# Issuing weight loads at the end of each turn, and three steps from scores to values in the first group

## The chip, the cores and the metric

One NeuronCore of a Trainium2 chip. The engines are TensorE (PE, with its weight loads as PEld), VectorE (DVE), ScalarE (ACT), GpSimd (POOL) and SyncE (SP), which in this kernel issues every DMA. The metric is the device time of one execution in microseconds (us); the program is run several times and the median is compared.

## What is computed

The reference is an attention layer followed by a feed-forward layer with two weight matrices.

- Attention: batch 4, 8 heads, 768 tokens, head size 64. Each query sees the keys at a distance under 16, and 24 summary keys, one per block of 32 keys (the maximum over the block; the summary value is the mean). A softmax runs over both kinds of scores together.
- Feed-forward: the heads' outputs give x of 3072 x 512; `h = x @ w_in` (512 x 2048), `g = h * tanh(softplus(h))` (the Mish function), and the result is `g @ w_out` (2048 x 512).

```python
scores_s = scale * np.einsum('bhsd,bhnd->bhsn', q, k_sum)
scores_s = scores_s + np.log(block)
scores_l_m = np.where(mask_l, scores_l, -1000000000.0)
scores_all = np.concatenate([scores_l_m, scores_s], axis=-1)
...
h = x @ w_in
sp = np.where(h > 20.0, h, np.log1p(np.exp(np.minimum(h, 20.0))))
g = h * np.tanh(sp)
return (g @ w_out).astype(np.float32)
```

## The kernel before

**Units.** The attention is cut into 48 units (`todo`, L393): 12 chunks of 256 tokens by 4 pairs of heads. A unit goes through these stages: its keys and queries are loaded (`att_load_keys`: DMA qk, L251, and a POOL copy of the summary keys into the same tile, L252); scores on PE (`att_scores`, L284 or L288/L290), minimum and mask on DVE (L299), exponentials on ACT (L304); `att_normalize` (DVE L313 and L314, POOL L315); `att_transpose` (PE L321, copied from PSUM to SBUF by ACT, L323, as tile pt, of which there is one); `att_values` (PE L339 into x_ps, then ACT splits off the high part xh, L340, and DVE the low part xl, L341). The values of a unit also need `att_load_values`: DMA vw from memory (L258) and a small DMA of the summary values vm into the same tile (L259). The qk tile and the vw tile have two buffers each, so the load for a unit waits on SP until the unit two before it has done its scores (qk) or its values (vw).

**Groups and steps.** The feed-forward layer works on groups of 512 tokens (8 units), 6 in all, each in 16 steps, one per 128 columns of w_in. In step i PE runs `ff_in` (12 matmuls, L353), ACT the Mish function (L360), ACT or DVE the split of its result into ah and al (L369, L371), and two steps later PE runs `ff_out` (12 matmuls, L381).

**Weights.** Weights arrive as 64-bit words, in 16 pieces of two 512 KB DMAs each (`load_weight`, L119), and are turned into a high and a low 32-bit part, piece by piece: `begin_weight` (ACT w_f, L143; DVE L144 and L145), `join_weight` (DVE L154 and L156), in the next turn `upper_weight` (ACT L129) and `lower_weight` (DVE L134). The stage tile that a piece is loaded into has two buffers, and L156 is the last that reads one: the next load but one waits for it. The tile w_f has one buffer, so `begin_weight` waits for the `lower_weight` of the piece before. Before the change `load_weight` is called as the last line of `join_weight`.

**Order.** The order of each engine's instructions is the order in which the program issues them (`manual_schedule`). A first loop of ten turns (u = 0 to 9) runs the attention of the first 8 units, with half of a weight piece per turn: `join_weight` in odd turns, `lower_weight` and `begin_weight` in even ones. In this loop a turn's loads of qk and vw stand after `join_weight`. Then the main loop runs the 96 steps of the feed-forward, with the next group's attention between them: in the first group (steps 0 to 15) the units stand at the even steps 0 to 12 and at step 13 (`at`), one whole weight piece is begun and joined per step up to step 10, and the values of a unit stand two steps after its scores. Steps 4, 6, 8 and 10 also take the key maximum for a new batch (`key_summary`, DVE L220), which frees a buffer for the load vsum (L199); the odd steps behind them reduce it (`value_summary`, DVE L240), send the result out (vm<-vq, L242) and load the next keys (ks, L195). vsum and ks share one buffer.

**PSUM.** From the main loop on, ph (`ff_in`), the two score tiles of a unit, x_ps and pt_ps rotate over the four buffers of one pool (`ps_w`). In the first loop x_ps and pt_ps use another pool.

Of the kernel before, what the change touches and what calls it, by code (L numbers as in the profile page):

```python
# [31 lines left out]
NFC = DFF // P  # L32
# [18 lines left out]
def _as_f32(bits):  # L51
    import struct
    return struct.unpack("<f", struct.pack("<I", bits))[0]
# [3 lines left out]
def fused_kernel(ctx: ExitStack, tc: tile.TileContext, q0, qk, kt, v0, vw, vs, w_in, w_out, out):  # L57
# [39 lines left out]
    def weight_tiles(pool, name, blocks):  # L97
        return [[pool.tile([P, blocks, WP], F32R, name=f"{name}_{w}_{part}") for part in ("hi", "lo")]
                for w in ("in", "out")]
# [14 lines left out]
    def load_weight():  # L114
        if weights:
            w, fc = weights.pop(0)
            t = stage.tile([P, WB, WP], I64, tag="stage", name=f"w{w}_{fc}")
            for k in range(WB):
                nc.sync.dma_start(t[:, k, :], (w_in, w_out)[w][fc + k])  # L119
            loaded.append((w, fc, t))  # L120
# [5 lines left out]
    def upper_weight():  # L126
        if joined:
            w, fc, f = joined[0]
            nc.scalar.copy(piece(w, 0, fc), f)  # L129

    def lower_weight():
        if joined:
            w, fc, f = joined.pop(0)
            nc.vector.tensor_sub(piece(w, 1, fc), f, piece(w, 0, fc).bitcast(F32))  # L134

    def begin_weight():

        if loaded:
            w, fc, t = loaded.pop(0)
            words = t.rearrange("p k f -> p (k f)").bitcast(U32).rearrange("p (f two) -> p f two", two=2)  # L140
            x, high = words[:, :, 0], words[:, :, 1]
            f = ff.tile([P, WB * WP], F32, tag="f", name=f"w{w}_{fc}_f", bufs=1)
            nc.scalar.activation(f, high.bitcast(F32), AF.Copy, scale=2.0 ** -OFFSET)  # L143
            nc.vector.tensor_scalar(out=x, in0=x, scalar1=29, scalar2=None, op0=ALU.logical_shift_right)  # L144
            nc.vector.scalar_tensor_tensor(out=x, in0=high, scalar=SIGN, in1=x,  # L145
                                           op0=ALU.bitwise_and, op1=ALU.bitwise_or)
            begun.append((w, fc, f, x))

    def join_weight():

        if begun:
            w, fc, f, x = begun.pop(0)
            u = f.bitcast(U32)
            nc.vector.tensor_scalar(out=f, in0=f, scalar1=-_as_f32(F32_MAX), scalar2=_as_f32(F32_MAX),  # L154
                                    op0=ALU.max, op1=ALU.min)
            nc.vector.scalar_tensor_tensor(out=u, in0=u, scalar=3, in1=x,  # L156
                                           op0=ALU.logical_shift_left, op1=ALU.bitwise_or)
            joined.append((w, fc, f))
            load_weight()


    begin = ExitStack()
# [30 lines left out]
    def load_key_source(b, hp):  # L193
        ks = sources[b, hp, 0] = stage.tile([P, S], F32, tag="sum", name=f"ks{b}_{hp}", bufs=1)
        nc.sync.dma_start(ks, kt[b, hp])  # L195
# [27 lines left out]
    def first_value_summary(hp):  # L223

        vm = att.tile([KA, P], F32, tag="vm", name=f"vm0_{hp}", bufs=HP)[KW:KA]
        summary[0, hp].append(vm)
        vwt, t = units[0, hp]["v"], units[0, hp]["rest"]
        ps = att_psum(0, f"vm_ps0_{hp}")
        for j in range(NQ + NR):
            nc.tensor.matmul(ps[KW:KA, 0:P], *((blocks[0:KW, j, :], vwt[0:KW, j, :]) if j < NQ else  # L230
                                               (blocks[:, j, :], t[:, j - NQ, :])),
                             start=(j == 0), stop=(j == NQ + NR - 1))
        nc.scalar.copy(vm, ps[KW:KA, 0:P])
        nc.sync.dma_start(vwt[KW:KA], vm.unsqueeze(1).broadcast_to([NB, NQ, P]))
# [20 lines left out]
    def att_load_values(c, hp):  # L255
        b = c // CPB
        vwt = att.tile([KA, NQ, P], F32, tag="vw", name=f"vw{c}_{hp}")
        nc.sync.dma_start(vwt[0:KW], vw[c, hp].rearrange("p (s k) -> p s k", s=NQ))  # L258
        nc.sync.dma_start(vwt[KW:KA], summary[b, hp][1].unsqueeze(1).broadcast_to([NB, NQ, P]))  # L259
        units[c, hp]["v"] = vwt  # L260

    def att_summaries(u):

        for i, f in ((u, value_summary), (u + 1, load_key_source)):
            if i < len(todo) and todo[i][0] % CPB == 0:
                f(todo[i][0] // CPB, todo[i][1])

    def att_psum(c, name, scores=False):

        pool, tag = (ps_o, "o") if c < CG and not scores else (ps_w, "w")  # L270
        return pool.tile([P, 512], F32, tag=tag, name=name)
# [45 lines left out]
    def att_transpose(c, hp):  # L317
        u = units[c, hp]
        ps = att_psum(c, f"pt_ps{c}_{hp}")
        for s in range(NQ):  # L320
            nc.tensor.transpose(ps[:KA, s * P:(s + 1) * P], u["p"][:, s, :], ident)  # L321
        pt = att.tile([KA, NQ, P], F32, tag="pt", name=f"pt{c}_{hp}", bufs=1)
        nc.scalar.copy(pt.rearrange("p s q -> p (s q)"), ps[:KA, :])  # L323
        u["pt"] = pt

    def att_values(c, hp):
        u = units.pop((c, hp))
        g, half = divmod(c, CG)
        if g not in xs:
            xs[g] = (xp.tile([P, HP, TG], F32R, tag="xh", name=f"xh{g}"),  # L330
                     xp.tile([P, HP, TG], F32R, tag="xl", name=f"xl{g}"))
        xh, xl = (x[:, hp, half * CH:(half + 1) * CH] for x in xs[g])
        ps = att_psum(c, f"x_ps{c}_{hp}")
        for s in range(NQ):
            for h in range(2):
                d = slice(h * D, (h + 1) * D)
                x = ps[d, s * QT:(s + 1) * QT]
                pt = u["pt"][:, h * NQ // 2 + s // 2, s % 2 * QT:(s % 2 + 1) * QT]
                nc.tensor.matmul(x, u["v"][:, s, d], pt, start=True, stop=True)  # L339
        nc.scalar.copy(xh, ps[:, :CH])  # L340
        return lambda: nc.vector.tensor_sub(xl, ps[:, :CH], xh.bitcast(F32))  # L341
# [51 lines left out]
    todo = [(c, hp) for c in range(NCH) for hp in range(HP)]  # L393
    steps = [(g, fc) for g in range(NG) for fc in range(NFC)]

    at = {}
    for u, unit in enumerate(todo[CG * HP:]):
        g, u = divmod(u, CG * HP)
# [17 lines left out]
    for u in range(n + 2):  # L416
        if u % 2 == 0:
            upper_weight()
        if u < n:
            att_scores(*todo[u])  # L420
        if u < HP:
            first_value_summary(u)
        lower = att_values(*todo[u - 2]) if 2 <= u else None
        if u % 2:
            join_weight()
        else:
            lower_weight()
            begin_weight()
        if u + 1 < HP:
            key_summary(0, u + 1, units[todo[u + 1]]["k"][:, WIN:])  # L430
        if lower:
            lower()
        if u == HP + 1:
            begin.close()
            late += weight_tiles(ctx.enter_context(tc.tile_pool(name="late", bufs=1)), "w_late", NFC - EARLY)
        if u < n:
            att_normalize(*todo[u])
        if HP - 2 <= u < n:
            att_load_keys(*todo[u + 2])
        if HP <= u:  # L440
            att_load_values(*todo[u])
        if 1 <= u <= n:
            att_transpose(*todo[u - 1])

    load_key_source(1, 0)
    waiting = []
    for i in range(len(steps) + 2):
        upper_weight()  # L450
        if i < len(steps):
            ff_in(*steps[i])
            ff_act(*steps[i])
            if i < NFC:
                waiting.append(ff_split(*steps[i]))
        if 0 < i <= NFC:
            waiting.pop(0)()
        lower_weight()
        lower = att_values(*at[i - 2]) if i - 2 in at else None
        if lower and i >= NFC:  # L460
            lower()
        if i in at:
            att_scores(*at[i])
        begin_weight()
        if lower and i < NFC:
            lower()
        if NFC <= i < len(steps):
            ff_split(*steps[i])()
        if i in at:
            att_normalize(*at[i])  # L470
        join_weight()
        if i in at:
            if todo.index(at[i]) + 2 < len(todo):
                att_load_keys(*todo[todo.index(at[i]) + 2])
        if i - 2 in at and todo.index(at[i - 2]) + 2 < len(todo):
            att_load_values(*todo[todo.index(at[i - 2]) + 2])
        if i - 1 in at:
            att_summaries(todo.index(at[i - 1]) + 2)
        if i >= 2:
            ff_out(*steps[i - 2])  # L480
        if i - 1 in at:
            att_transpose(*at[i - 1])
# [44 lines left out]
```

## Time and profile before

| | before |
|---|---|
| median of 3 runs | 690.5 us (688.78 to 691.71) |
| profiled execution, its own time | 691.24 us |
| its span, first to last instruction | 689.5 us |
| mean granted TensorE clock | 0.967 |
| PE busy | 641.1 us (93%) |
| DVE, ACT, POOL busy | 290.6, 332.9, 68.1 us |
| chain that ended last, by engine | PE 79%, DMA 6%, ACT 6%, DVE 5% |
| DMA | 71.05 MB, mean 103 GB/s |

Times within the span count from its first instruction. An idle time is put down to what released the engine last; idle time of an engine off the chain costs nothing. A granted clock of 1.00 is 2.4 GHz, 0.50 is 1.2 GHz; a value between them is a mean over the stretch. SPq is SP's queue: its rows are the issues of DMAs, not their transfers, and an issue that must wait for an engine holds all issues behind it.

### The profile page before, as it was taken

How to read it: one execution, taken by the hardware profiler on the slowest of the kernel's cores; microseconds unless marked ns; L12 is line 12 of the kernel's file. 1: busy time of each engine (PE TensorE's matmuls, PEld its weight loads, DVE VectorE, ACT ScalarE, POOL GpSimd, SP SyncE). 2: the span in 40 equal slices, each digit the busy share in tenths (PEclk: the TensorE clock that was granted, in tenths of full speed). 3: DMA queues.
4: the chain of work that ended last, by engine and by line, in shares of the span. 5: the costliest groups of instructions: out<-in, count | busy, mean ns of one | idle time of the engine just before them, and what ended most of it. 6: DMA issues, size and time to landing. Idle time of an engine off the chain costs nothing.

```text
span 689.5 us, 10881 instructions
## 1 busy us (share of the span) xinstructions
PE 641.1 (93%) x4160; PEld 513.9 (75%) x4160; DVE 290.6 (42%) x836; ACT 332.9 (48%) x722; POOL 68.1 (10%) x119
## 2 busy tenths in 40 slices
PE   4845798879999999999999999999999999999997
PEld 3634576667778878878878878878788788888886
DVE  3866889895223225453232244442242232221112
ACT  2655776668555445454554554454464454111111
POOL 3121011021101001001001001001001000000000
PEclk9866899999999999999999999999999999999999
DMA  8776455744232122542112134432141110010001
GB/s 281 197 259 217 153 190 212 213 152 141 59 106 87 45 67 92 158 153 89 45 48 85 44 130 114 134 113 68 45 140 54 45 59 0 1 62 0 1 1 61
DMA packets 31253, 71.05 MB, mean 103 GB/s; under 512 B 4833, under 2 KB 9953, under 8 KB 31201
## 3 DMA queue, kind: packets, MB, share of 16 engines
q1 hardware_dynamic: 31200, 70.35, 31.9%
q8 instruction: 33, 0.54, 0.3%
q14 instruction: 20, 0.16, 0.1%
HBM read 61.54 MB, written 6.29 MB: 98 GB/s over the span
## 4 chain that ended last, share of the span: by engine, by line
PE 79%; DMA 6%; ACT 6%; DVE 5%; issue 2%; SPq 1%; POOL 0%; POOLq 0%; ACTq 0%; DVEq 0%
PE po L381 35%; PE ph L353 34%; PE x_ps L339 4%; PE sc L284 3%; PE pt_ps L321 3%; DVE w_f L156 2%; DMA vsum<-vs 2%; DMA q<-q 1%; DMA v<-v 1%; DVE w_f L154 1%; ACT w_f L143 1%; DMA qk<-qk 1%; ACT pr L304 1%; DMA vw<-vm 1%; ACT L360 1%
## 5 line engine op out<-in xcount | busy, mean ns | idle before, releaser
L360 ACT ACTIVATE a<-ph 128x512 f32<-128x512 f32 x96 | 57.4, 598 | 155.4 <-PE ph L353 155.0
L369 DVE CAST ah<-a 128x512 fp32r<-128x512 f32 x80 | 34.0, 425 | 197.1 <-ACT a L360 197.1
L353 PE MATMUL ph<-xh,w_early_in_hi 128*128 128x512 f32 x240 | 97.8, 407 | 0.0
L381 PE MATMUL po<-w_early_out_hi,ah 128*128 128x512 f32 x240 | 97.5, 406 | 0.0
L360 ACT ACT_TABLE_LOAD x41 | 52.6, 1283 | 88.6 <-PE ph L353 88.4
L353 PE MATMUL ph<-xh,w_early_in_lo 128*128 128x512 f32 x240 | 94.9, 396 | 0.0
L353 PE MATMUL ph<-xl,w_early_in_hi 128*128 128x512 f32 x240 | 94.8, 395 | 0.0
L381 PE MATMUL po<-w_early_out_lo,ah 128*128 128x512 f32 x240 | 94.3, 393 | 0.0
L381 PE MATMUL po<-w_early_out_hi,al 128*128 128x512 f32 x240 | 94.1, 392 | 0.0
L315 POOL TENSOR_TENSOR pr<-pr,rs 128x480 f32<-128x480 f32 x48 | 49.2, 1026 | 394.9 <-DVE rs L314 327.5
L304 ACT ACTIVATE pr<-pr,nm 128x120 f32<-128x120 f32 x192 | 73.5, 384 | 16.8 <-DVE nm L299 16.3
L341 DVE TENSOR_TENSOR xl<-x_ps,xh 128x256 fp32r<-128x256 f32 x48 | 20.3, 423 | 119.8 <-ACT xh L340 119.8
L371 DVE TENSOR_TENSOR al<-a,ah 128x512 fp32r<-128x512 f32 x96 | 66.3, 691 | 2.8
L381 PE MATMUL po<-w_late_out_hi,ah 128*128 128x512 f32 x144 | 58.0, 403 | 0.0
L353 PE MATMUL ph<-xh,w_late_in_hi 128*128 128x512 f32 x144 | 57.6, 400 | 0.0
L381 PE MATMUL po<-w_late_out_lo,ah 128*128 128x512 f32 x144 | 56.3, 391 | 0.0
L353 PE MATMUL ph<-xh,w_late_in_lo 128*128 128x512 f32 x144 | 56.2, 391 | 0.0
L353 PE MATMUL ph<-xl,w_late_in_hi 128*128 128x512 f32 x144 | 56.1, 390 | 0.0
L381 PE MATMUL po<-w_late_out_hi,al 128*128 128x512 f32 x144 | 56.0, 389 | 0.0
L381 PEld LDWEIGHTS po<-w_early_out_hi,ah 128*128 128x128 f32 x240 | 45.7, 190 | 13.1 <-issue 4.4
L339 PEld LDWEIGHTS x_ps<-pt,vw 120*64 120x64 f32 x768 | 29.0, 149 | 33.5 <-issue 18.5
L353 PEld LDWEIGHTS ph<-xh,w_early_in_lo 128*128 128x128 f32 x240 | 45.8, 191 | 10.2
(74 smaller groups left out, 934.5 us busy)
## 6 DMA issues: line engine op xcount, KB each, us to landing
qk<-qk SPq DMA_DIRECT2D x44, 496.0 KB
vw<-vw SPq DMA_DIRECT2D x48, 192.0 KB
w<-w_in SPq DMA_DIRECT2D x16, 512.0 KB
w<-w_out SPq DMA_DIRECT2D x16, 512.0 KB
ks<-kt SPq DMA_DIRECT2D x17, 384.0 KB
out<-o SPq DMA_DIRECT2D x24, 256.0 KB
vsum<-vs SPq DMA_DIRECT2D x12, 384.0 KB
vw<-vm SPq DMA_DIRECT2D x48, 48.0 KB
```

Source lines behind the costliest of these rows:

```text
L156: nc.vector.scalar_tensor_tensor(out=u, in0=u, scalar=3, in1=x, op0=ALU.logical_shift_left, op1=ALU.bitwise_or)
L284: nc.tensor.matmul(ps[h][row, at0:at0 + KA], u["qk"][r, s, h * QT:(h + 1) * QT], u["qk"][r, s, P:], start=True, stop=True)
L304: nc.scalar.activation(pr[:, s, :], pr[:, s, :], AF.Exp, scale=-1.0, bias=nm[:, s:s + 1], accum_out=sm[:, s:s + 1])
L315: nc.gpsimd.tensor_mul(pr, pr, rs.unsqueeze(2).broadcast_to([P, NQ, KA]))
L321: nc.tensor.transpose(ps[:KA, s * P:(s + 1) * P], u["p"][:, s, :], ident)
L339: nc.tensor.matmul(x, u["v"][:, s, d], pt, start=True, stop=True)
L341: return lambda: nc.vector.tensor_sub(xl, ps[:, :CH], xh.bitcast(F32))
L353: nc.tensor.matmul(ph, w[:, cc * P:(cc + 1) * P], x[:, cc, :], start=(cc == 0 and n == 0), stop=(cc == NCC - 1 and n == 2))
L360: nc.scalar.activation(a, st[g, fc], AF.Mish)
L369: (nc.scalar.copy if g == 0 else nc.vector.tensor_copy)(ah, a)
L371: return lambda: nc.vector.tensor_sub(al, a, ah.bitcast(F32))
L381: nc.tensor.matmul(po[g][t], a[:, tok], w, start=(fc == 0 and n == 0), stop=(fc == NFC - 1 and n == 2))
```

## The change

`load_weight()` is taken out of `join_weight` and called at the end of each odd turn of the first loop, and in each step of the main loop after the loads of keys, values and summaries and ahead of `ff_out`. The values of the units at steps 0 to 10 of the first group are issued three steps after their scores (steps 3, 5, ... 13), and with them the load of the values two units on. The units at steps 12 and 13, and those of all later groups, keep two steps.

```diff
--- before.py
+++ after.py
@@ -156,7 +156,6 @@
             nc.vector.scalar_tensor_tensor(out=u, in0=u, scalar=3, in1=x,
                                            op0=ALU.logical_shift_left, op1=ALU.bitwise_or)
             joined.append((w, fc, f))
-            load_weight()
 
 
     begin = ExitStack()
@@ -441,9 +440,12 @@
             att_load_values(*todo[u])
         if 1 <= u <= n:
             att_transpose(*todo[u - 1])
-
-
-
+        if u % 2:
+            load_weight()
+
+
+
+    values = {i + (3 if i < NFC - 4 else 2): unit for i, unit in at.items()}
     load_key_source(1, 0)
     waiting = []
     for i in range(len(steps) + 2):
@@ -456,7 +458,7 @@
         if 0 < i <= NFC:
             waiting.pop(0)()
         lower_weight()
-        lower = att_values(*at[i - 2]) if i - 2 in at else None
+        lower = att_values(*values[i]) if i in values else None
         if lower and i >= NFC:
             lower()
         if i in at:
@@ -472,10 +474,11 @@
         if i in at:
             if todo.index(at[i]) + 2 < len(todo):
                 att_load_keys(*todo[todo.index(at[i]) + 2])
-        if i - 2 in at and todo.index(at[i - 2]) + 2 < len(todo):
-            att_load_values(*todo[todo.index(at[i - 2]) + 2])
+        if i in values and todo.index(values[i]) + 2 < len(todo):
+            att_load_values(*todo[todo.index(values[i]) + 2])
         if i - 1 in at:
             att_summaries(todo.index(at[i - 1]) + 2)
+        load_weight()
         if i >= 2:
             ff_out(*steps[i - 2])
         if i - 1 in at:
```

## Rows read from the trace of the kernel before

**Rows 1.** Time by stretches: busy us per engine (count), clock, DMA share, GB/s.
```profile
62.00:66.00 4.00, 4.00 (x13) 3.12 (x11) 1.65 (x2) 2.60 (x3) 0.00 (x0) 0.50 1.00 355
60.00:160.00 100.00, 83.58 (x494) 65.82 (x496) 81.84 (x144) 69.17 (x121) 11.23 (x12) 0.90 0.56 184
160.00:180.00 20.00, 20.00 (x144) 15.90 (x144) 6.91 (x28) 13.41 (x30) 3.60 (x5) 1.00 0.34 100
```

**Rows 2.** SP's own waits, 0 to 62 us: line, releaser, total, times, longest.
```profile
SPq L119 <- DVE w_f L156: 16.9, 3, 7.4
```

**Rows 3.** Timeline of PE, DVE, ACT, POOL, turns 2 to 9: start, length, instruction.
```profile
29.46 0.27 POOL L252 COPY qk<-km 128x96 f32<-128x96 f32 x1 [1.57 <-DMA qk<-qk]
...
36.69 0.18 DVE L314 RECIPROCAL rs<-rs 128x4 f32<-128x4 f32 x1
...
37.93 0.26 POOL L252 COPY qk<-km 128x96 f32<-128x96 f32 x1 [4.71 <-DMA qk<-qk]
...
38.25 1.18 PE L284 MATMUL sc<-qk 64*64 64x120 f32 x16 [4.33 <-POOL qk L252]
...
40.09 0.27 POOL L252 COPY qk<-km 128x96 f32<-128x96 f32 x1 [0.95 <-DMA qk<-qk]
...
42.78 0.28 DVE L299 CUSTOM_DVE_ANT_0 pr<-sc,base 128x120 f32<-128x120 f32 x1
...
47.36 0.18 DVE L314 RECIPROCAL rs<-rs 128x4 f32<-128x4 f32 x1
...
49.11 0.26 POOL L252 COPY qk<-km 128x96 f32<-128x96 f32 x1 [5.14 <-DMA qk<-qk]
...
50.53 1.12 PE L339 MATMUL x_ps<-pt,vw 120*64 120x64 f32 x16
...
50.74 0.28 DVE L299 CUSTOM_DVE_ANT_0 pr<-sc,base 128x120 f32<-128x120 f32 x1 [3.21 <-PE sc L284]
...
57.48 0.58 ACT L323 COPY pt<-pt_ps 120x512 f32<-120x512 f32 x1
...
61.08 1.12 PE L339 MATMUL x_ps<-pt,vw 120*64 120x64 f32 x16 [5.09 <-DMA vw<-vm]
```

**Rows 4.** The chain that ended last, merged: start, length, piece.
```profile
62.21 5.00 PE ph L353 x12
...
119.74 1.90 DVE w_f L156
...
138.02 1.90 DVE w_f L156
...
164.15 2.72 PE ph L353 x12
```

**Rows 5.** Timeline of SP and DVE, steps 6 to 8.
```profile
121.56 0.94 DVE L220 TENSOR_REDUCE km<-ks 128x24 f32<-128x768 f32 x1
...
121.71 1.62 SPq L119 DMA_DIRECT2D w<-w_out  x2
...
130.94 1.22 DVE L240 TENSOR_REDUCE vq<-vsum 96x32 f32<-96x1024 f32 x1 [2.61 <-DMA vsum<-vs]
...
134.84 0.69 DVE L144 TENSOR_SCALAR w<-w 128x1024 uint32<-128x1024 uint32 x1
```

**Rows 6.** Timeline of SP, turns 2 to 7: DMA issues.
```profile
25.74 0.51 SPq L251 DMA_DIRECT2D qk<-qk  x1
...
31.52 0.94 SPq L119 DMA_DIRECT2D w<-w_out  x2
...
43.27 0.33 SPq L251 DMA_DIRECT2D qk<-qk  x1
...
55.38 0.82 SPq L259 DMA_DIRECT2D vw<-vm  x1
```

**Rows 7.** Timeline of DVE and PE, steps 3 and 4.
```profile
93.28 1.23 DVE L145 SCALAR_TENSOR_TENSOR w<-w 128x1024 uint32<-128x1024 uint32 x1
...
95.52 0.69 PE L339 MATMUL x_ps<-pt,vw 120*64 120x64 f32 x16 [1.15 <-ACT pt L323]
```

## Prediction before the run

> **What bounds the kernel now.** I read the page's slices first, then the time by stretches, then the chain, and only then single queues. In the time by stretches [rows 1] the reader is to see two kernels. From 160 us on TensorE (PE) is busy 20.00 of 20.00 us at clock 1.00, and the same holds nearly to the end: what is left at 160 us is a fixed amount of PE work, and a change that only reorders loads can't shorten it. Before that, PE is idle 100 - 83.58 = 16.4 us of the stretch from 60 to 160, and much of the time before 60. So the change is worth just as much as it lets PE reach its closed stretch earlier.
>
> What holds the start? SP's own waits [rows 2]: in the first 62 us SP stood 16.9 us at line 119, the weight load, waiting for the join (DVE line 156) that still reads the stage buffer. SP issues in order, so the qk, vw and vm loads of a turn stood behind that wait, and then behind the weights' 1 MB. Their consumers are the gaps [rows 3]: on PE 4.33 us in front of the scores of unit 5, and 5.09 us in front of the last values (61.08), which waited for vw<-vm. A third belongs to unit 7, whose km copy on POOL came at 49.11, after 5.14 us of waiting for its qk.
>
> From 75 to 157 us the chain [rows 4] holds no PE: it goes round ScalarE (ACT: weight's upper half, Mish with its table, exps, w_f) and VectorE (DVE: L154, L156), one weight piece a step. From join to join, two steps take 138.02 - 119.74 = 18.28 us at their longest; that pair holds DVE's 2.61 us wait for vsum [rows 5].
>
> **Edit 1: weight loads last in the turn.** Each load is two DMAs of 512 KB; the pair takes SP 0.94 us to issue in turn 3 [rows 6]. It is moved past qk, vw, vm, and in the main loop also past vsum, vm<-vq and ks, all on SP; the POOL queue is moved past nothing, but its km copies sit in order between the normalizations, so a late qk there holds a normalization too. Turn by turn, units counted from 0:
> - Unit 5 (turn 3). Its qk takes the weights' place at 31.5. A qk with no weights just ahead of it was copied 29.46 - 25.74 = 3.72 us after issue [rows 3, 6], so the copy moves from 37.93 to 35.2. Scores take 1.18 us and end at 36.7, when DVE comes free of the reciprocal at 36.69 + 0.18.
> - Unit 6 (turn 4). The bytes in front of its qk are the same ones in another order, so its copy stays at 40.09; scores run from 40.36 to 41.54, and DVE starts on them at 41.54, not 42.78: 1.24 us gained. Its reciprocal ended at 47.54, 4.76 us after that start; now at 46.3.
> - Unit 7 (turn 5). Its qk was issued at 43.27, behind the join. Now it only waits for unit 5's scores (its buffer), so it goes out at 36.7. Even one lone-load time after unit 6's copy it is there at 43.8, before DVE is free at 46.3. DVE starts at 46.3, not 50.74: 4.44 us gained.
> - Last values (turn 9). They need pt of unit 7 and vw<-vm. The pt copy ended at 57.48 + 0.58 = 58.06; less 4.44 that is 53.6. The vm load waits for values of unit 5, which ended at 50.53 + 1.12 = 51.65, now 47.2; with the 0.9 us that two issues ahead of it cost (an estimate from the 0.94 for two in turn 3) it goes out at 48.1, and with the same 5.7 us from issue to use (61.08 - 55.38) it is there at 53.8. So the values start near 53.7, and ff_in behind them: **7.4 us** earlier than 61.08.
>
> Ends for this term: 1.2 us if only unit 6's gain lasts and the other gaps come back under another name; 14.6 us if all three gaps (4.33 on PE, 5.14 taken at POOL's copy, 5.09) went. I take 7.4, which follows the rows hop by hop.
>
> In the main loop edit 1 lets vsum go out before the weights, right after DVE's key maximum that frees its buffer. In the long pair vsum came in at 130.94, 9.2 us after the weight pair ahead of it was issued at 121.71 [rows 5]. Without that 1 MB it should be in before DVE asks, 2.61 us earlier than it came: **2.6 us** off the chain. Ends: 0, if another wait of that size follows, and 2.6, all that the row has. What is late next is the weight itself: behind vsum and qk it lands by the same 9.2 us, counted from the end of the key maximum, 121.56 + 0.94 = 122.5, so at 131.7. DVE's L144 wants it at 134.84 - 2.61 = 132.2. It holds with half a microsecond to spare; every other load has less in front of it. In odd steps the load also waits for vq on DVE, so a late vsum would hold it as well. If that cover goes, each microsecond of lateness is one on the chain.
>
> **Edit 2: values three steps after scores.** No instruction is added. x_ps, xh, xl and the vw load go from even to odd steps: xh leaves ACT's even step and enters the odd one, so the pair keeps its length. vw still has four steps before it is read. On PE the wait in front of values (1.15 us at 95.52, until ACT's pt copy) [rows 7] vanishes, but PSUM's four rotating buffers make a new one: an even step's second score buffer is the one x_ps had, free only after xl, which follows DVE's L145 (93.28 + 1.23 = 94.5, and xl itself on top). So the new wait ends shortly before 95.52, at the same point of PE's work and with the same work behind it. I take **0**. Ends: +7 us if six such waits of 1.15 us went without a successor, and -3.5 us if in six odd steps an ACT copy of 0.58 us (as that at 57.48) came onto the chain and left nothing in the even ones. The nearest row is that of the rotation, so 0.
>
> **Sum.** 7.4 + 2.6 + 0 = 10.0 us. The profiled execution took 691.24 us (span 689.5, the rest around it); it lies 0.7 us above the median 690.5. So 681.2 against its own time, and 680.5 as the median.
>
> **The clock, row against page.** The first ff_in took 5.00 us for twelve matmuls; a later one takes 2.72 [rows 4]. The granted clock there was 0.50, so 1.2 GHz, after PE had idled 5.09 us [rows 1, 3]. I keep 5.00 in the sum, since PE stays thinly used in the turns. The Trainium skill, TensorE: Matmul & The Clock Gate, section "HAM oscillation — how this bites in real kernels", says that waits for DMA between bursts are what drop PE to half clock, and that closing them keeps it up. By that rule 5.00 would become 2.72 and the sum 12.3. No row of before shows that stretch with the gaps closed.
>
> **Rivals.**
> - *The clock stays at 2.4 GHz into the first ff_in*: 2.28 us more, 678.2. For: two of the gaps go. Against: PE was granted 0.50 after a gap of this size, and smaller gaps stay. 12%.
> - *The main loop gives part back.* The weights come late at the vsum steps, by a microsecond or two each, and vsum's 2.6 us is swapped for them; or vm of unit 7 comes later than 53.8. Only 4 to 6 us remain: about 685. For: the spare is half a microsecond. 18%.
> - *The loads are not what holds the turns* (the change does nothing that counts): DVE, busy 4.76 us from a unit's start to its reciprocal, takes up the gaps. Within 0.5%, 690. Against: the waits name the DMA, not DVE [rows 2, 3]. 8%.
> - *Slower: the weights become the bound.* Place: ACT's w_f and DVE's L144 in steps 2 to 10, waiting for loads issued in steps 0 to 8. With nine loads each late by d, the chain grows by 9d. It beats the 10.0 us from d = 1.1, and at d = 1.6 the kernel takes 690.5 - 10 + 14.4 = 695. For: the load now stands behind up to three transfers and, in odd steps, behind vq. Against: the 9.2 us of the worst stretch fit into the time between join and L144, and the steps without vsum move less. 7%.
>
> **How the numbers follow.** The forecast with its sizes off by 2 us has 55%, the clock 12%, the partial gain 18%, none 8%, slower 7%. About 0.5% (3.45 us) is what a measurement here can tell from no change. Faster: 55 + 12 + 18 = 85%. The range reaches from 676.5 (clock, and first term 1.7 us larger) to 686.5 (partial gain, low end); outside lie the last two cases and a few per cent of the sizes.
>
> **What would show it.** Right: the first ff_in starts near 54 us; no PE gap of over 4 us in front of scores or values after 30 us; SP's line 119 still waits but nothing is behind it; DVE's wait for vsum at step 8 under 0.5 us; PE closed from about 150 us. Wrong: ff_in still near 60 us (first term), DVE or ACT waiting for DMA w (weights late), PE's gaps in front of scores longer than those in front of values were (rotation), or a later start of the closed stretch than the first ff_in's gain tells.

## The result and the profile after

The changed kernel takes 682.13 us (median of 4 runs, 680.79 to 683.15) where the kernel before takes 690.31 (4 runs, 688.78 to 691.71): a ratio of 0.9881 with a 95% interval of 0.9854 to 0.9908. The profiled execution of it took 682.29 us, with a span of 680.6. Behind the end of `join_weight` the line numbers after are one lower than before (scores L283, values L338, `ff_in` L352, `ff_out` L380); the weights' own lines, the join's L156 among them, are the same.

**Where the 8.9 us of span went.** They can be cut at four marks of PE: the scores of unit 4, the first `ff_in`, the start of the 401st of the 2304 feedforward matmuls (well inside the closed stretch), and the last of them. Between the last two marks both traces need 489.98 us: PE's closed stretch is worth the same. What differs lies before it.

The timeline of PE before, at the first mark, and its granted clock shortly before:

```profile
20.00:30.00 10.00, 8.92 (x112) 6.99 (x105) 7.44 (x25) 5.39 (x21) 2.24 (x3) 0.66 0.75 215
...
31.43 0.64 PE L284 MATMUL sc<-qk 64*64 64x120 f32 x16
```

The stretch from 20 to 30 us of the changed kernel, its first `ff_in`, two of the stretches of [rows 1], and two short passages of the main loop (columns as there: busy us and count of PE, PEld, DVE, ACT, POOL, then clock, DMA share, GB/s):

```profile
20.00:30.00 10.00, 8.43 (x150) 6.75 (x142) 9.00 (x31) 7.35 (x25) 2.70 (x4) 1.00 0.74 206
54.00:58.00 4.00, 4.00 (x11) 3.12 (x10) 2.33 (x3) 2.33 (x2) 0.00 (x0) 0.50 0.72 207
60.00:160.00 100.00, 88.91 (x525) 68.08 (x524) 84.56 (x160) 73.05 (x131) 12.17 (x14) 0.91 0.53 176
160.00:180.00 20.00, 20.00 (x132) 15.97 (x131) 5.29 (x19) 12.00 (x29) 2.92 (x4) 1.00 0.29 87
...
88.00:93.00 5.00, 5.00 (x14) 3.96 (x15) 4.46 (x13) 4.53 (x10) 0.00 (x0) 0.58 0.61 211
150.00:154.50 4.50, 4.50 (x13) 3.57 (x14) 3.12 (x14) 4.45 (x11) 1.33 (x2) 0.62 0.47 139
```

And its timeline through the turns, with SP's issues between (start, length, engine, instruction, idle time before and releaser):

```profile
29.03 0.64 PE L283 MATMUL sc<-qk 64*64 64x120 f32 x16
...
29.20 0.51 SPq L250 DMA_DIRECT2D qk<-qk  x1
...
29.81 0.84 SPq L119 DMA_DIRECT2D w<-w_out  x2
...
30.84 0.33 SPq L250 DMA_DIRECT2D qk<-qk  x1
...
33.64 0.33 POOL L251 COPY qk<-km 128x96 f32<-128x96 f32 x1 [2.82 <-DMA qk<-qk]
34.02 1.16 PE L283 MATMUL sc<-qk 64*64 64x120 f32 x16 [2.50 <-POOL qk L251]
...
39.03 0.26 POOL L251 COPY qk<-km 128x96 f32<-128x96 f32 x1 [3.43 <-DMA qk<-qk]
39.34 0.74 PE L283 MATMUL sc<-qk 64*64 64x120 f32 x16 [2.07 <-POOL qk L251]
...
41.88 0.51 POOL L251 COPY qk<-km 128x96 f32<-128x96 f32 x1 [1.64 <-DMA qk<-qk]
...
44.76 0.28 DVE L298 CUSTOM_DVE_ANT_0 pr<-sc,base 128x120 f32<-128x120 f32 x1
...
48.63 1.12 PE L338 MATMUL x_ps<-pt,vw 120*64 120x64 f32 x16 [1.49 <-DMA vw<-vm]
...
52.37 1.12 PE L338 MATMUL x_ps<-pt,vw 120*64 120x64 f32 x16 [1.58 <-ACT pt L322]
```

SP's own waits of the first 62 us, to be laid beside [rows 2], the three longest:

```profile
SPq L119 <- DVE w_f L156: 8.4, 3, 6.6
SPq L250 <- PE sc L283: 8.2, 4, 3.0
SPq L257 <- PE x_ps L338: 5.0, 4, 2.4
```

To be seen: the weight load now goes out behind the qk of unit 5 (29.81 after 29.20), the gaps of 4.33, 5.14 and 5.09 us of [rows 3] are 2.50, 1.64 (POOL's, at unit 7's copy) and 1.58, and the last values wait for ACT's copy of pt, no longer for a load. New is the gap at unit 6, where POOL waits 3.43 us in place of 0.95 and PE 2.07. SP now also stands 8.2 us for scores and 5.0 for values, waits for the qk and vw buffers that the kernel before didn't have. From the scores of unit 4 to the last values it is 52.37 - 29.03 = 23.34 us, against 61.08 - 31.43 = 29.65 before: 6.31 us. Another 2.40 us are gained ahead of the scores of unit 4 (31.43 to 29.03), with a clock of 1.00 in place of 0.66 from 20 to 30 us; that part isn't safely the change's ("What stays open", below). From the first `ff_in` to the 401st matmul it is 133.16 us before and 132.93 after: 0.2 us. The sum, 2.4 + 6.3 + 0.2, is the 8.9 us.

That the main loop shows only 0.2 us goes with this execution's clock. Its chain holds, behind the qk of unit 6 (first line), these pieces of twelve matmuls:

```profile
30.84 8.04 DMA qk<-qk
...
53.49 5.11 PE ph L352 x12
...
87.98 4.92 PE po L380 x12
...
96.26 2.95 PE po L380 x12
...
149.99 4.55 PE po L380 x12
```

Twice in the main loop a piece of `ff_out` took long, 4.92 and 4.55 us in place of some 2.95, at a granted clock of 0.58 and 0.62 (the last two stretches above). In the chain of a second profile of the same kernel (below, span 678.2) both are gone, and the same stretch takes 130.59 us, 2.3 less.

DVE and PE in the steps of [rows 5], after:

```profile
86.92 1.07 PE L283 MATMUL sc<-qk 64*64 64x120 f32 x14 [2.01 <-ACT pt L322]
...
111.68 1.22 DVE L156 SCALAR_TENSOR_TENSOR w_f<-w_f,w 128x1024 uint32<-128x1024 uint32 x1
...
119.77 1.21 DVE L239 TENSOR_REDUCE vq<-vsum 96x32 f32<-96x1024 f32 x1
...
127.63 1.23 DVE L156 SCALAR_TENSOR_TENSOR w_f<-w_f,w 128x1024 uint32<-128x1024 uint32 x1
```

The reduction of vsum has no idle time before it any more, and the long pair of steps takes 127.63 - 111.68 = 15.95 us, not 18.28. PE's gap has moved from values to scores, which [rows 7] had in front of x_ps.

### The profile page after: what moved, and what is told of

Its sections match the earlier page's. It is cut to its first block, busy times and chain, and to the rows that moved or that the text cites. A ratio compares the mean times of both kernels' runs of the same rounds, so it can differ in the third digit from the quotient of the medians.

```text
span 680.6 us, 10882 instructions
## 1 busy us (share of the span) xinstructions
PE 644.6 (95%) x4160; PEld 514.8 (76%) x4160; DVE 291.1 (43%) x836; ACT 333.4 (49%) x722; POOL 67.5 (10%) x119
## 4 chain that ended last, share of the span: by engine, by line
PE 82%; ACT 8%; DVE 4%; DMA 3%; issue 1%; SPq 0%; POOL 0%; POOLq 0%; ACTq 0%; DVEq 0%
PE po L380 37%; PE ph L352 35%; PE x_ps L338 4%; PE sc L283 3%; PE pt_ps L320 3%; ACT w_f L143 2%; DVE w_f L156 2%; DVE w_f L154 1%; DMA qk<-qk 1%; ACT pr L303 1%; DMA vw<-vm 1%; DMA vw<-vw 1%; ACT L359 1%; ACT L303 1%; ACT a L359 1%
## 5 line engine op out<-in xcount | busy, mean ns | idle before, releaser
L380 PE MATMUL po<-w_early_out_hi,ah 128*128 128x512 f32 x240 | 98.6, 411 | 0.0
L352 PE MATMUL ph<-xh,w_early_in_hi 128*128 128x512 f32 x240 | 97.8, 407 | 0.0
L380 PE MATMUL po<-w_early_out_lo,ah 128*128 128x512 f32 x240 | 95.3, 397 | 0.0
L352 PE MATMUL ph<-xl,w_early_in_hi 128*128 128x512 f32 x240 | 95.0, 396 | 0.0
L352 PE MATMUL ph<-xh,w_early_in_lo 128*128 128x512 f32 x240 | 94.9, 395 | 0.0
L380 PE MATMUL po<-w_early_out_hi,al 128*128 128x512 f32 x240 | 94.7, 394 | 0.0
L380 PE MATMUL po<-w_late_out_hi,ah 128*128 128x512 f32 x144 | 58.5, 407 | 0.0
L352 PE MATMUL ph<-xh,w_late_in_hi 128*128 128x512 f32 x144 | 57.6, 400 | 0.0
L380 PE MATMUL po<-w_late_out_lo,ah 128*128 128x512 f32 x144 | 57.0, 396 | 0.0
L380 PE MATMUL po<-w_late_out_hi,al 128*128 128x512 f32 x144 | 56.8, 394 | 0.0
L352 PE MATMUL ph<-xh,w_late_in_lo 128*128 128x512 f32 x144 | 56.2, 391 | 0.0
L352 PE MATMUL ph<-xl,w_late_in_hi 128*128 128x512 f32 x144 | 56.1, 390 | 0.0
L380 PEld LDWEIGHTS po<-w_early_out_hi,ah 128*128 128x128 f32 x240 | 45.9, 191 | 13.0 <-issue 4.1
L352 PEld LDWEIGHTS ph<-xh,w_early_in_lo 128*128 128x128 f32 x240 | 46.0, 192 | 10.2
L380 PEld LDWEIGHTS po<-w_early_out_lo,ah 128*128 128x128 f32 x240 | 45.8, 191 | 10.3
```

What stands on the lines that cost most here:

```text
L352: nc.tensor.matmul(ph, w[:, cc * P:(cc + 1) * P], x[:, cc, :], start=(cc == 0 and n == 0), stop=(cc == NCC - 1 and n == 2))
L380: nc.tensor.matmul(po[g][t], a[:, tok], w, start=(fc == 0 and n == 0), stop=(fc == NFC - 1 and n == 2))
```

## The experiments

Every kernel differs from the changed one, or from the one named, by the lines shown. "Turns" is the time from the scores of unit 4 to the last values in its profile: 29.65 us before, 23.34 after. The medians of the kernel before in these comparisons were 689.3 to 689.7 us.

**The edits one by one.** The first four kernels put back one piece or two each.

Loads last in both loops, but values two steps after scores:

```diff
-    values = {i + (3 if i < NFC - 4 else 2): unit for i, unit in at.items()}
+    values = {i + 2: unit for i, unit in at.items()}
```

> Edit 1 alone: weight loads last in both loops, values two steps after scores as before. Theory of the prediction: the loads carry all of the gain, edit 2 is worth 0, so about 682 us (8 us under the kernel before), first ff_in near 53 to 54 us, no DVE wait for vsum over 0.5 us in step 8. Rival (PE gains from the values being later): at least 4 us of the 8 are missing, 686 or more.

680.32 us, ratio 0.9879 (0.9857 to 0.9901), turns 53.02 - 29.16 = 23.86. Within the intervals that is the whole gain of the change.

Values three steps after scores, but loads in their old place:

```diff
             join_weight()
+            load_weight()
...
-        if u % 2:
-            load_weight()
...
         join_weight()
+        load_weight()
...
-        load_weight()
```

> Edit 2 alone: weight loads at the join as before, values three steps after scores at steps 0 to 10. Theory: 0, within 1.5 us of 690.3; PE waits for ACT's pt copy in front of scores instead of in front of values, by the same few us in all. Rival (edit 2 is what pays): 686 or less. Rival (it costs, since xh enters the odd step): 692 or more.

688.68 us, 0.9997 (0.9983 to 1.0011). PE, in the turns and in two steps of the main loop:

```profile
31.17 0.64 PE L283 MATMUL sc<-qk 64*64 64x120 f32 x16
...
61.32 0.98 PE L338 MATMUL x_ps<-pt,vw 120*64 120x64 f32 x13 [4.88 <-DMA vw<-vm]
...
95.46 0.63 PE L283 MATMUL sc<-qk 64*64 64x120 f32 x14 [2.01 <-ACT pt L322]
...
126.79 0.63 PE L283 MATMUL sc<-qk 64*64 64x120 f32 x14 [2.02 <-ACT pt L322]
```

The turns are those of before (30.15). PE's waits for ACT's copy of pt, 1.15 to 2.83 us in front of five of the six values of before (one in [rows 7]), stand in front of scores now, 0.47 to 2.02 us. DVE's wait for vsum is also shorter here, 1.23 us in place of 2.61, but the time doesn't show it: edit 2 by itself is worth nothing.

Loads last in the first loop alone (values after two steps, and in the main loop `load_weight()` right behind `join_weight()`):

> The weight load moved to the end of the turn in the first loop only; main loop and values as before. Theory: the first term, 6 to 7.5 us, so 683 to 684.5; first ff_in near 54, DVE still waits some 2.6 us for vsum. Rival (a good part of the 8.7 us at the first ff_in of the changed kernel's profile is its start before any moved instruction, 2.4 us at the scores of unit 4): 4 to 6.3 us, 684 to 686.5.

680.96 us, 0.9890 (0.9868 to 0.9913), turns 53.36 - 30.11 = 23.25. The median is 2 us better than the lower end of what was expected (683); the profiled execution (684.10) was the slowest of the six.

Loads last in the main loop alone (values after two steps, and in the first loop `load_weight()` right behind `join_weight()`):

> The weight load moved last in the main loop only; first loop and values as before. Theory: the second term, 2 to 2.6 us, about 688; first ff_in near 62 as before; DVE's wait for vsum at step 8 gone. Rival (the closed stretch of PE starts no earlier, since the gain is given back at the clock or in PE's order): within 1 us of 690.3.

687.79 us, 0.9973 (0.9956 to 0.9990). Its timeline:

```profile
29.52 0.64 PE L283 MATMUL sc<-qk 64*64 64x120 f32 x16
...
59.14 1.12 PE L338 MATMUL x_ps<-pt,vw 120*64 120x64 f32 x16 [4.71 <-DMA vw<-vm]
...
129.52 0.70 DVE L144 TENSOR_SCALAR w<-w 128x1024 uint32<-128x1024 uint32 x1 [0.32 <-DMA w<-w_out]
```

The turns are long again (29.62). The main loop's loads alone bring 1.9 us by the ratio (0.7 to 3.0 by its interval); on top of the first loop's they bring 680.96 - 680.32 = 0.6, which these runs can't tell from 0 nor from 1.9. DVE waits once for weights, 0.32 us.

The changed kernel once more, unedited, for a second profile:

> The changed kernel once more, on the chip of the next three. Theory (edit 2 worth 0): the ratio of the runs with edit 1 alone, 0.988, within 0.002. Rival (edit 2 costs on top of edit 1, as its chain from first ff_in to the last join is 1.7 us longer in the profile): 0.990 or more.

680.37 us, 0.9869 (0.9843 to 0.9894). Scores of unit 4 at 28.98, last values at 52.34, so turns of 23.36; then 130.59 us to the 401st matmul. By the same four marks the gain of 11.3 us of span is 2.4 + 6.3 + 2.6.

**SP's wait or the megabyte?** In the old order the keys stood behind SP's wait for the join and behind 1 MB of weights. The next kernel is the one with the loads moved in the first loop alone, with a 4-byte transfer in the load's old place that needs the join's result: SP waits as before, but for no bytes.

```diff
         if u % 2:
             join_weight()
+            nc.sync.dma_start(small.tile([P, 1], F32, tag="gate", name=f"gate{u}")[0:1], joined[-1][2][0:1, 0:1])
```

> As the run with the weight loads moved in the first loop only, but a DMA of 4 bytes that reads the join's result stands in the old place, so SP still waits there for the join in turns 3, 5, 7 and 9, while the 1 MB goes out last. Theory A (SP's wait in front of qk and vw is what cost): most of the gain goes, within 3 us of the kernel before, 687 or more; from scores of unit 4 to the last values 28 us or more. Theory B (the 1 MB ahead in the rings is what cost): the gain stays, 683 or less, 24.5 us or less. Both: between, about 26 us.

689.57 us, 1.000 (0.9983 to 1.0017): by its time, the wait would be everything. By its trace it isn't: the turns take 55.82 - 30.89 = 24.93 us, and the 401st feedforward matmul starts at 189.53, 5.8 us ahead of the kernel before. The gain is lost later, where nothing of the edit is left: from the 289th to the 2201st feedforward matmul it needs 502.43 us, against 497.95 in the kernel with the loads moved in the first loop and 497.96 in the one before. No gap shows there; late in the span the matmuls stand 0.231 us apart in place of 0.227.

What the gate also did: its four buffers of 32 bytes moved the tiles allocated behind them (the first loop's inputs, the activations' pool with ah and al, the late weights) up by 128 bytes on each partition. In all other kernels of this section, save the first below and the two of the next heading, they lie where they lie in the kernel before. Two kernels part the two things. The first has the loads moved in the first loop, no gate, and the gate's buffers kept:

```diff
+    nc.gpsimd.memset(small.tile([P, 1], F32, tag="gate", name="gate"), 0.0)
```

> The kernel with the load moved in the first loop only, without any gate transfer, but with the gate's buffers kept reserved (four slots of 32 bytes on each partition; one memset of GpSimd behind the last loop writes one of them), so that the activations' tiles (pool ff) and the late weights lie 128 bytes higher than in every other kernel but wait_without_bytes. In wait_without_bytes the feedforward matmuls from the 700th on stood 0.230 us apart in place of 0.227, without a gap, and the last 1900 of them took 502.4 us in place of 498.0, long after the last gate. Theory P (places): the 128 bytes do that. Then the last 1900 feedforward matmuls take some 502.4 us here, and the time is 681.0 + 4.4 = 685.4 us (683.5 to 687). Theory D (the transfers or what else they change in the program do it): 498.0 us and 681 us.

688.22 us, 0.9975 (0.9957 to 0.9993), turns 51.88 - 29.17 = 22.71, and 502.42 us from the 289th to the 2201st matmul. The matmuls are as expected; the median lies 1.2 us above the expected range, and what that is was not traced. The second has the gate, with the places of all tiles but its own and rs's kept:

```diff
-        rs = small.tile([P, NQ], F32, tag="rs", name=f"rs{c}_{hp}")
+        rs = small.tile([P, NQ], F32, tag="rs", name=f"rs{c}_{hp}", bufs=3)
...
+            nc.sync.dma_start(small.tile([P, 1], F32, tag="gate", name=f"gate{u}", bufs=1)[0:1], joined[-1][2][0:1, 0:1])
```

> wait_without_bytes again (the load last, and in the old place of it a 4-byte transfer on SP that needs the join's result), but with one gate buffer and three of the four buffers of the reciprocals' sums, so that all other tiles lie where they lie in the other kernels. Theory P: the last 1900 feedforward matmuls take 498.0 us again, the turns some 25 us as in wait_without_bytes, and the time is 689.6 - 4.4 = 685.2 us, of which what is over 681.0 us (load moved in the first loop only) is what SP's wait alone costs. Theory D: 502.4 us and 689.6 us again. In both, were the wait alone the whole of the loss, the turns would take 29.7 us; were it the megabyte's bytes alone, 23.3 us and 681 us.

684.61 us, 0.9923 (0.9895 to 0.9950), and 497.96 us for the same matmuls. So the places slow the matmuls, not the gate. Its turns:

```profile
30.04 0.64 PE L283 MATMUL sc<-qk 64*64 64x120 f32 x16
...
54.88 1.12 PE L338 MATMUL x_ps<-pt,vw 120*64 120x64 f32 x16 [1.94 <-DMA vw<-vm]
```

24.84 us. Of the 6.3 us that the turns gain, SP's wait (with the issue of the gate itself) takes back 1.5, and the megabyte ahead of the keys has the other 4.8. These are single profiles: in the eight with the loads last in the odd turns and no gate, the turns take 22.71 to 23.86 us, so the wait's share lies between 1.0 and 2.1. In the medians the wait costs 684.61 - 680.96 = 3.65 us, though the two intervals overlap; what the 2 us beyond the turns are was not traced.

**How far the places matter.** Two more shifts of the same tiles: 256 bytes ([P, 16] in the first kernel's memset) and 32 bytes (`bufs=1` there).

> places_only with the reserved slots four times 64 bytes: the same tiles (first loop's inputs, the activations of pool ff, the late weights) lie 256 bytes higher than in the kernel with the load moved in the first loop only, in place of 128. Theory Q (what counts is where the tiles lie against some coarser step, and 256 bytes are a whole number of it): the last 1900 feedforward matmuls take 498 us and the time is 681 us. Theory R (any shift from the places of the kernel before costs): 502.5 us and 685 to 688 us.

682.62 us, 0.9894 (0.9873 to 0.9915), and 497.95 us from the 289th to the 2201st matmul: as with no shift.

> places_only with one reserved slot of 32 bytes: the same tiles lie 32 bytes higher. Theory Q: 32 bytes are a fraction of the step, so the last 1900 feedforward matmuls are slowed, to 502.5 us if any misplacement costs the same, by a quarter of that (499 us) if it goes with the distance; time 682 to 688 us. Theory R: 502.5 us and 685 to 688 us. Should the rows stand at 498 us and the time at 681 us, the 128 bytes are a case by themselves and the rule stays open.

688.01 us, 0.9984 (0.9967 to 1.0001), and 503.56 us. Groups of PE between 186 and 676 us (operation, tiles, count, busy us, mean ns), first unshifted:

```profile
L380 PE MATMUL po<-w_early_out_hi,al 128*128 128x512 f32 x200 | 77.8, 389 | 0.0
...
L352 PE MATMUL ph<-xl,w_early_in_hi 128*128 128x512 f32 x192 | 74.8, 390 | 0.0
...
L380 PE MATMUL po<-w_late_out_hi,al 128*128 128x512 f32 x121 | 47.1, 389 | 0.0
...
L352 PE MATMUL ph<-xl,w_late_in_hi 128*128 128x512 f32 x120 | 46.8, 390 | 0.0
```

Shifted by 128 bytes:

```profile
L380 PE MATMUL po<-w_early_out_hi,al 128*128 128x512 f32 x200 | 78.9, 394 | 0.0
...
L352 PE MATMUL ph<-xl,w_early_in_hi 128*128 128x512 f32 x192 | 74.8, 390 | 0.0
L352 PE MATMUL ph<-xl,w_late_in_hi 128*128 128x512 f32 x120 | 47.3, 394 | 0.0
...
L380 PE MATMUL po<-w_late_out_hi,al 128*128 128x512 f32 x116 | 45.2, 390 | 0.0
```

The same groups with all shifts, mean ns, and which of the two operands has moved:

| group | moved | unshifted | 128 bytes | 32 bytes | 256 bytes |
|---|---|---|---|---|---|
| al with early weights | al | 389 | 394 | 395 | 389 |
| xl with late weights | weights | 390 | 394 | 395 | 390 |
| al with late weights | both | 389 | 390 | 391 | 389 |
| xl with early weights | neither | 390 | 390 | 390 | 390 |

Slow are the matmuls of which one operand has moved and the other hasn't, in `ff_out` and in `ff_in`; where both have moved together, they are nearly as fast as before. So what costs is not where a tile lies, but that the two operands of a matmul are shifted against each other. Three shifts fit a step of 256 bytes; that any fraction of it costs, or why, they don't show.

**Other ways to order the loads, and the clock.** Loads at the end of even turns in the first loop, with edit 1 otherwise:

```diff
-        if u % 2:
+        if u in (2, 4, 6, 8, 9):
             load_weight()
```

> Edit 1 alone, but in the first loop the weight pieces go out at the end of turns 2, 4, 6, 8 and 9, so that the qk of unit 6 stands in front of a piece too. Theory: PE's wait for that qk (2.07 us in the changed kernel) and the one for vw<-vm of unit 6 (1.5 to 2.7) go, 1 to 2 us better than edit 1 alone, 678.5 to 679.5. Rival: DVE is the bound there already or a weight piece comes late in turns 4 to 8: no gain, 680 or more.

680.41 us, 0.9860 (0.9835 to 0.9885), turns 51.38 - 29.36 = 22.02, a DVE wait of 0.50 us for weights at 123.44. By its time it can't be told from the changed kernel, 0.9869 beside the same runs: the 1 to 2 us that were expected show in the turns of the profile (1.8 us under those of edit 1 alone) and not in the median.

Extra work for PE in the first group, to see what its clock is worth:

```diff
+        if CG <= c < 2 * CG and (c, hp) != (CG, 0):
+            for k in range(6):
+                nc.tensor.matmul(ps[0], early[0][0][:, 0, 0:P], xs[0][0][:, 0, :], start=True, stop=True)
```

> The changed kernel with six matmuls of 128 x 512 more, thrown away (their tile is overwritten by the scores), in front of the scores at steps 2 to 13, where PE stood up to 2 us for ACT's pt copy. Theory (edit 2's shorter gaps are given back at half clock: ff_out took 4.9 and 4.6 us behind them, not 2.7 to 3.0): clock 1.00 from 84 us on, 1.5 to 3.5 us better than the changed kernel, about 679.5. Rival (the clock is not what holds it): no better than the changed kernel, or worse by up to seven times 1.4 us where there was no gap to fill.

682.56 us, 0.9901 (0.9876 to 0.9926). The time by stretches:

```profile
60.00:160.00 100.00, 93.71 (x566) 71.40 (x565) 83.77 (x156) 74.00 (x139) 12.15 (x14) 0.98 0.52 177
```

The clock is 0.98 in place of 0.91 and the time is no better, where 1.5 to 3.5 us were expected. Whether the six matmuls of each step take what the clock gives, or the clock had nothing to give here, this run doesn't part.

## Why the prediction was right, step by step

The forecast was 680.5 us, the two medians are 682.13 and 680.37; the sum was 10.0 us, the gains are 8.2 and 9.3. That the total came so close is in part luck: in the two profiles the stretches that the forecast has terms for, the turns and the main loop, give 6.3 + 0.2 and 6.3 + 2.6 us of the 8.9 and 11.3 us of span. The remaining 2.4 lie ahead of the turns, where the forecast has no term.

**Term 1, the turns: the mechanism held, its 7.4 us measured 6.3.** Laid over the times of before (2.40 us added to every time after), the hops are:

| hop | forecast | measured |
|---|---|---|
| qk copy of unit 5 | 35.2 | 33.64 + 2.40 = 36.04 |
| qk copy of unit 6 | 40.09 | 39.03 + 2.40 = 41.43 |
| DVE's start on unit 7 | 46.3 | 44.76 + 2.40 = 47.16 |
| last values | 53.7 | 52.37 + 2.40 = 54.77 |

The first miss is the lone-load time: unit 5's qk took 33.64 - 29.20 = 4.44 us from issue to copy, not 3.72. The megabyte goes out 0.6 us behind it, but that isn't shown to be the cause: in the gate kernel with unmoved tiles, with the megabyte 0.4 us behind it, the same qk took 3.62. The second is the sentence that the bytes in front of unit 6's qk "are the same ones in another order", so that its copy stays. They are, but that qk, now directly behind them, took 39.03 - 30.84 = 8.19 us from issue to copy (8.04 of it in the chain), where it took 6.98 before (40.09 less its issue at 33.11), and its copy comes 1.34 us later than forecast. In the other nine profiles with the first loop's loads moved to odd turns it took 7.14 to 7.98; why it is longer was not traced. At unit 7 the miss is 0.86 us, at the last values 1.07, and pt of unit 7 is what the values wait for, not vm; the forecast had the two 0.2 us apart, vm the later one (53.6 and 53.8).

The forecast held SP's wait and the bytes behind it together. The gate kernel with unmoved tiles parts them: 1.5 us for the wait, 4.8 for the bytes.

**Term 2, vsum: 2.61 us forecast, 2.33 measured in the long pair, 1.9 (0.7 to 3.0) as a time by itself.** On top of term 1 its share is not resolved. The forecast's reading of the chain, that from 75 to 157 us it goes round ACT and DVE, left out that the load of vsum itself stood in it twice:

```profile
123.43 7.49 DMA vsum<-vs
...
140.89 5.84 DMA vsum<-vs
```

In the chain of the changed kernel from 50 to 175 us there is no load. The cover that was named is as thin as it was said to be: DVE waits for weights 0.32 and 0.50 us in two of the kernels, and not at all in the profile of the changed one. One vsum wait stays in the kernels with the main loop's loads moved and values after two steps (1.85 us at 154.89 in the one with those loads alone); by then PE's closed stretch has begun (154.62). With values after three steps as well it is 0.16 us at most.

**Term 3, edit 2: 0 forecast, 0 measured, by another releaser.** The prediction let the second score tile wait for x_ps's buffer, free after xl. The rows name ACT's copy of pt (2.01 us at 86.92): the buffer that comes round is pt_ps's. The argument that counted, the same point of PE's work with the same work behind it, holds.

**The clock.** The first `ff_in` took 5.11 us, and 4.40 in the second profile, where 5.00 was kept in the sum: PE's waits behind DMA in the turns had shrunk to 2.50, 2.07 and 1.49 us, and the clock from 54 to 58 us was still 0.50. The Trainium skill, TensorE: Matmul & The Clock Gate, section "HAM oscillation — how this bites in real kernels", says that with the waits for DMA out of the way PE stays at full clock, from which the prediction made 2.72 us. The waits here were shortened, not closed, so the runs don't put that to the full test; shortening them didn't do it. In the main loop, where the extra matmuls kept PE busy, the clock was 0.98, which is in line with the page.

**The rivals.** That the weights become the bound is out (no wait for them over 0.50 us). That the loads are not what holds the turns is out too (0.9890 with the first loop's loads alone). That the main loop gives part back, because weights come late, is out by the same waits; its 0.2 us in the first profile goes with two passages near half clock, which the second profile's chain doesn't have. That the clock rises ahead of the first `ff_in` is out with 5.11 us, and with 4.40 it shows 0.6 us of its 2.28.

**What stays open.** The medians give the first loop's loads 8.4 us, the turns 6.3. Ahead of the turns, the scores of unit 4 start at 28.9 to 30.1 us in nine of eleven profiles with that edit, but at 30.89 and 32.19 in the other two, and at 29.52, 31.17 and 31.43 in the three without it. The early starts go with a clock of 1.00 from 20 to 30 us, the late ones with 0.85 or 0.66, on either side. The edit also moves a load of the second turn, so it may have a part in this; no run tells which.

## What to carry to other kernels

On a queue that issues in order, bytes that are needed late can cost those behind them more than a wait does (here 4.8 us against 1.5): put the bulk load behind the small loads that the next unit asks for, and price it by which load then stands directly behind the bulk. A wait that goes from one consumer of a rotating buffer to another was worth nothing here (0.9997), with the same work of PE behind it.

A probe that adds a tile moves other tiles. Before its time is read, compare the matmuls of a stretch that the probe can't touch; here 4.5 us of a "cost of the wait" were places. And a reading by groups needs all of them: the early weights alone would have put the cost on al.

## What the runs showed that was not expected

Moving ah, al and the late weights up by 32 or 128 bytes on each partition made the 1912 feedforward matmuls from the 289th on take 503.56 and 502.42 us, against 497.95 with 256 bytes or none, at a granted clock of 1.00 and with no gap in front of any. The slow ones are those with one operand moved and the other not (394 to 395 ns in place of 389 to 390). Against the kernel with the first loop's loads alone the medians rose by some 7 us, against the shift by 256 bytes by 5.4 and 5.6; the matmuls show 5.6 and 4.5. The Trainium skill, SBUF — State Buffer, section "Operand start alignment", asks for multiples of the element's size and says that this is "about legality, not speed"; the runs are in line with the first (all these places are multiples of 32 bytes) and add a price to the second, which goes by where the two operands lie to each other.
